# Transformer block on one core: where the last weight pieces stand in the load queue, and o's and LN2's transposes one visit later

## The chip, the core and the metric

One Trainium2 chip, one of its cores. The time is device microseconds (us) for one run of the whole program, from inputs in HBM to the output in HBM. Matmuls run on TensorE (PE, with its weight loads PEld), elementwise work on VectorE (DVE) and ScalarE (ACT), a few small operations on GpSimd (POOL); SyncE (SP) issues nearly all transfers. A transfer issued by SP goes to one queue over 16 DMA engines.

## The reference

S = 2048 rows of D = 576, 32 heads of 18, MLP width F = 4608, bfloat16 inputs.

```python
def _A_ref(x, wqkv, wo):
    qkv = (x @ wqkv).reshape(B, S, 3, H, Dh)            # q, k, v
    idx = pos[:, None] - (arange(8) * 2)[None, :]         # 8 keys, two rows apart, causal
    logits = einsum("bhsd,bhswd->bhsw", q, k[idx]) * Dh ** -0.5   # -1e9 where idx < 0
    return einsum("bhsw,bhswd->bhsd", softmax(logits), v[idx]).reshape(B, S, D) @ wo

def _B_ref(x, w1, b1, w2, b2):
    return gelu(layernorm(x) @ w1 + b1) @ w2 + b2

h = x + _A_ref(layernorm(x), wqkv, wo)
h2 = h + _B_ref(layernorm(h), w1, b1, w2, b2)
```

## The kernel before

**Tiles.** Row p*16 + j of x lies in partition p of tile j, so the 16 tiles of 128 rows are strided, and the keys of a tile are whole other tiles of the same parity (with the first rows taken from one partition further up, the "halo"). EVEN is tiles 0, 2, ... 14, ODD is 1, 3, ... 15. Attention runs over A = 14, 12, 10, 8, 6, 4, 2, 0, 15, ... in pairs (GROUPS): 14 and 12 are the first MLP group, 10 and 8 the second.

**A visit.** PE works in visits. One visit computes two "duos", a duo being the product of one tile with 576 columns. Each has a first phase (10 matmuls of 64 rows, in which two halves of the array take the two halves of the rows) and a second (8 matmuls with the halves exchanged). `visit` (L242) runs the first phases of all duos, then `hook`, then for each duo its second phase, its evacuation (`evac`, on ACT), and what `between` gives for it. Between the two phases of a duo stands a `marker` (L237): a nop on POOL that waits for the last matmul of the first phase, and for which the second phase waits. The PSUM pairs of the duos turn in a ring of three (tags C, A, B); the fourth, D, is for transposes and for W_o.

**The QKV stage.** 24 visits, numbered qd = 0 to 23, take `seq`: K and V and Q of the even tiles, then of the odd ones. `hooks[qd]`, `between[qd]`, `after[qd]` and `loads[qd]` (L937 to L983) say what each engine gets around a visit. The order on every engine is the order in which the code calls things (manual_schedule), so an entry moved in these tables is moved in the engines' queues. `wo_with` puts W_o's product of a tile into a visit as a third duo, in D.

**What is interleaved.** For tiles 14 and 12, attention is finished inside this stage: products of q with 8 K tiles (`att_qk_a`, L352, one DVE operation of 2.5 us), sums over the head dimension (`att_qk_add`, L361, four halvings), logits, maximum (`att_max`), exp on ACT, probabilities (`att_den`), products with V (`att_pv_a`, L407) and their sums (`att_pv_b`, L413, L414) into q_all, which then holds o. `halo(j, 1)` and `halo(j, 2)` (L347) reload a K or V tile of kv_ring, shifted, from DRAM once the products of tile j have read it; the products of the next tile read it too. `o_tail` copies o's last 64 columns on ACT, `tr_o` (L431) transposes o on PE, W_o's product follows, and `ln2` (h = x + W_o's product, statistics; DVE), `ln2_rstd` (the power −1/2, POOL, L161), `ln2_norm` (ACT, L539 and L174) and `tr_h` (PE, copied to hnT on ACT, L557) prepare the MLP's input hnT. For tiles 10 and 8, o goes out to DRAM and is read back transposed (`dma_tr_o`: L210, L211, L216) during the first MLP.

**Odd x.** Normalised odd tiles are written to q_all by ACT, sent out two at a time (`out_x`, L292 and L293) and read back transposed (`in_x`, L296) into xnT: read i serves tiles ODD[2i] and ODD[2i+1], visits 12 + 3i to 14 + 3i.

**Weights.** W1 comes in six pieces of 768 columns (768 KB each, `load_w1`), W_o in four pieces (`load_wo`, two transfers each), W2 in seven (`load_w2`) with the row blocks of 128 in the tuple. The last W2 block, rows 28 to 35, is w2b_sb. Every `load` waits for the last evacuation that was recorded before it (`pace`), and they all stand in SP's one queue with the stores and the transposed reads. The MLP visits of group 0 use W1's pieces in pairs: 0 and 1 in its visits 0 and 1, 2 and 3 in 1 and 2, 4 and 5 in visit 3.

**MLP.** For group 0 (`k == 0`, L1046 to L1056), `m1[v]` is called ahead of MLP visit v, `mid` within it, `ia[f]` and `ib[f]` ahead of row f of the second product (L603), for the first and the second tile. W_o's product for tile 10 (c) is the late duo of visit 3; that of tile 8 (d) stands at row 19 of the second product.

At the start PE multiplies constants (L833) so that it is not idle while x and the first weights come.

Of the kernel before, what the change touches and what calls it, by code (L numbers as in the profile page):

```python
# [17 lines left out]
def kernel(  # L18
# [12 lines left out]
    nc = tc.nc  # L31
    P = 128
# [11 lines left out]
    FA = 28  # L44
# [51 lines left out]
    def psum_pair(tag, name, dtype=F32):  # L96
        n = 512 if dtype == F32 else 1024
        return psum.tile([P, 2, n], dtype, tag=f"ps{tag}", name=name)
# [36 lines left out]
    def load_w2(c):  # L135
        f0, f1 = (0, 4, 7, 11, 14, 21, FA, FT)[c:c + 2]
        dst = w2a_sb[:, f0:f1, :] if f1 <= FA else w2b_sb[:]
        load(dst, B_w2[f0 * P:f1 * P, :].rearrange("(ft p) c -> p ft c", p=P))
# [79 lines left out]
    def half_rows(r):  # L218
        return slice(r * HP, (r + 1) * HP)
# [138 lines left out]
    def att_qk_add(j, steps):  # L358
        for o, a, c in steps:
            n = (c - a if c < 9 else 9) * H  # L360
            nc.vector.tensor_tensor(out=prod[:, :, o * H:o * H + n], in0=prod[:, :, a * H:a * H + n],  # L361
                                    in1=prod[:, :, c * H:c * H + n], op=ALU.add)

    def att_qk_b(j, i, skip=0):
        side[j] = i
        out = logit_of([j])[:, 0]
        att_qk_add(j, ((0, 0, 9), (0, 0, 4), (0, 0, 2), (0, 0, 1))[skip:])
        nc.vector.tensor_tensor(out=out, in0=prod[:, :, 0:H], in1=prod[:, :, 8 * H:9 * H], op=ALU.add)
        if j // 2 + 1 < W:
            nc.vector.memset(out[0:1, j // 2 + 1:W, :], -1e9)  # L370
# [332 lines left out]
    def c_(fn, *a):  # L703
        return lambda: fn(*a)
# [100 lines left out]
    with tc.manual_schedule(engines={ENG.PE, ENG.Activation, ENG.DVE, ENG.SP, ENG.Pool}):  # L805
# [26 lines left out]
        for n in [512] * 8 + [P] * 5:  # L832
            nc.tensor.matmul(busy[:, 0, 0:n], lhsT=ones[:, 0:P], rhs=ones[:, 0:n], start=True, stop=True)  # L833
# [104 lines left out]
        for c, v in enumerate((2, 3, 4, 13, 13, 17)):  # L938
            loads[v] = loads.get(v, []) + [c_(load_w1, c)]
        for q, v in enumerate((6, 8, 11, 12)):  # L940
            loads[v] = [c_(load_wo, [q])]
        for n, v in enumerate((19, 19, 20, 20, 21, 22)):
            loads[v] = loads.get(v, []) + [c_(load_w2, n)]
# [15 lines left out]
            13: [c_(ln1_act, 10, 1), c_(in_x, 2), c_(out_x, 3), c_(store_halo, A[2]), c_(store_halo, A[3])],  # L959
            14: [c_(att_pv, A[1]), c_(in_x, 3), c_(load, b2_bc, B_b2.partition_broadcast(P))],  # L960
            15: [c_(halo, A[1], 2), c_(o_tail, A[0])],
            17: [c_(o_tail, A[1]), c_(ln2, A[0]), c_(att_qk_a, A[2])],
            18: [c_(ln2_rstd, A[0]), c_(halo, A[2], 1)],
            19: [c_(ln2, A[1])],
            20: [c_(ln2_rstd, A[1]), c_(att_qk_rest, A[2], 0)],
# [4 lines left out]
            18: {1: [c_(tr_o, A[1], "D")]},  # L970
            19: {1: [c_(ln2_norm, A[0])]},
            21: [c_(ln2_norm, A[1])],
            22: [c_(att_exp, A[2])],
        }
        wo_with = {17: A[0], 19: A[1]}
# [5 lines left out]
            21: c_(tr_h, A[0], "D"),  # L981
            22: c_(tr_h, A[1], "D"),
# [6 lines left out]
        tr_x(EVEN[0], "D")  # L989
        for qd in range(len(seq) // 2):  # L990
            duos = [qkv_duo(*seq[2 * qd]), qkv_duo(*seq[2 * qd + 1])]
            if qd in wo_with:
                duos.append(wo_duo(wo_with[qd], "D"))
            visit(duos, hooks.get(qd), between.get(qd, ()), apart=qd == 0)
            call(after.get(qd, ()))
            call(loads.get(qd, ()))
# [37 lines left out]
        for k, g in enumerate(GROUPS):  # L1034
# [11 lines left out]
            if k == 0:  # L1046
                m1[0] += [c_(halos, 1), c_(load_w2, 6), c_(att_qk_a, d), c_(att_qk_rest, d, 1), c_(halo, d, 1)]
                mid[0] = {1: [c_(exps, d)]}
                m1[1] = [c_(pv_t, c), c_(pv_t, d), c_(add_b2, g[0]), c_(add_b2, g[1]), c_(att_qk_a, e), c_(halo, e, 1)]
# [109 lines left out]
```

## Time and profile before

| | |
|---|---|
| time, median of 3 | 361.98 us (361.90, 361.98, 363.82) |
| profiled execution | 362.23 us, span 360.4 us, granted clock 0.995 |
| PE busy | 352.6 us, 98% of the span |
| DVE busy | 295.9 us, 82% |
| ACT busy | 235.9 us, 65% |
| HBM | 23.38 MB read, 12.42 MB written, 99 GB/s over the span |
| QKV stage | to 68.15 us, the first matmul of the MLP |
| MLP group 0 | 68.15 to 106.3 us |

The windows view gives, for a stretch a:b, its length, then the busy time of PE, PEld, DVE, ACT and POOL with the number of instructions, the granted share of the TensorE clock, the busy share of the DMA engines and the rate in GB/s. The chain that ended last is PE for 80% of the span; the rest is DVE 11%, DMA 5%, ACT 2%:

| engine, line | what | share of the span |
|---|---|---|
| PE L228 | MLP's first product | 39% |
| PE L691 | second product, groups 2 to 7 | 25% |
| PE L603 | second product, groups 0 and 1 | 10% |
| PE L228 | W_o | 4% |
| DMA | transposed read of odd x (xnT) | 3% |

### The profile page before, as it was taken

Reading aid. Unit: us, or ns where it says so; the run is one execution under the profiler, and the core shown is the slowest. Engines: PE = TensorE matmul, PEld = TensorE weight load, DVE = VectorE, ACT = ScalarE, POOL = GpSimd, SP = SyncE. Lnnn points to the kernel's source line nnn. Section 1 sums busy time; section 2 is a strip of 40 time slices with the busy share of each in tenths; the row PEclk is TensorE's granted clock in tenths of the full one; section 3 lists DMA queues with packets and bytes.
Section 4 is the critical chain, followed back from the end, with each engine's and each line's share of the span. In section 5 each row is a group of like instructions: output and inputs, shape, how many; then the busy total and the mean of one; then the engine's idle time right before and its main releaser. Section 6 shows DMA issues by size and latency. Waiting matters only on the chain.

```text
span 360.4 us, 11550 instructions
## 1 busy us (share of the span) xinstructions
PE 352.6 (98%) x4938; PEld 290.7 (81%) x4938; DVE 295.9 (82%) x416; ACT 235.9 (65%) x524; POOL 48.1 (13%) x61
## 2 busy tenths in 40 slices
PE   7999998999999999999999999999999999999996
PEld 3788886788778877887788778877887788778874
DVE  5999999989889998998799899989998989520431
ACT  4889764898556783668656956695669566706620
POOL 2340005000212020201110202021102110210000
PEclk8999999999999999999999999999999999999999
DMA  7996599972636496732463355344545254283001
GB/s 240 329 294 193 147 258 310 367 253 55 169 66 100 132 244 109 129 79 51 91 102 90 85 124 84 90 86 120 88 90 99 58 85 58 54 120 51 4 1 34
DMA packets 63492, 46.29 MB, mean 128 GB/s; under 512 B 32192, under 2 KB 61760, under 8 KB 63440
## 3 DMA queue, kind: packets, MB, share of 16 engines
q1 hardware_dynamic: 59472, 41.50, 43.6%
q0 software_dynamic: 3744, 3.84, 9.9%
q8 instruction: 38, 0.62, 0.8%
q10 hardware_dynamic: 224, 0.22, 0.3%
q14 instruction: 14, 0.11, 0.1%
HBM read 23.38 MB, written 12.42 MB: 99 GB/s over the span
## 4 chain that ended last, share of the span: by engine, by line
PE 80%; DVE 11%; DMA 5%; ACT 2%; issue 1%; SPq 0%; DVEq 0%; ACTq 0%
PE pm L228 39%; PE po L691 25%; PE po L603 10%; PE pw L228 4%; DMA xnT<-xd 3%; DVE ln_stats L148 2%; DVE prod L361 2%; DVE prod L407 1%; DVE prod L352 1%; PE pq L228 1%; DMA x_all<-in_A_x_dram 1%; DMA wq_sb<-in_A_wqkv_dram 1%; ACT h_all L584 1%; DVE prod L413 1%; DVE ln_mv L149 1%
## 5 line engine op out<-in xcount | busy, mean ns | idle before, releaser
L228 PE MATMUL pm<-hnT,w_sb 64*128 64x256 bf16 x2304 | 143.0, 269 | 0.0
L584 ACT ACTIVATE h_all<-pm,b_sb 128x256 f16<-128x256 f32 (+1 forms) x288 | 108.7, 496 | 51.0 <-PE pm L228 50.3
L228 PEld LDWEIGHTS <-w_sb 64*128 64x128 bf16 x2304 | 111.6, 94 | 15.2 <-issue 1.7
L228 PE MATMUL pq<-wq_sb,xnT 64*128 64x288 bf16 x720 | 55.7, 286 | 3.0 <-DMA xnT<-xd 1.8
L691 PEld LDWEIGHTS <-h_all 128*128 128x128 f16 x480 | 46.2, 98 | 13.7 <-issue 1.6
L228 PEld LDWEIGHTS <-xnT 64*128 64x128 bf16 x864 | 44.7, 95 | 11.9 <-DMA xnT<-xd 2.1
L361 DVE TENSOR_TENSOR prod<-prod 128x2304 bf16<-128x2304 bf16 (+1 forms) x64 | 44.2, 691 | 2.1
L352 DVE TENSOR_TENSOR prod<-kv_ring,q_all 128x4608 bf16<-128x4608 bf16 x16 | 40.8, 2551 | 3.2 <-POOL ln_rstd L498 2.4
L407 DVE TENSOR_TENSOR prod<-kv_ring,probs 128x4608 bf16<-128x4608 bf16 x16 | 40.9, 2558 | 2.2 <-DMA kv_ring<-kv_dram 1.7
L228 PE MATMUL pm<-hnT,w1h_sb 64*128 64x256 bf16 x288 | 39.2, 269 | 0.0
L691 PE MATMUL po<-w2a_sb,h_all 128*128 128x288 bf16 (+1 forms) x262 | 35.9, 286 | 0.0
L413 DVE TENSOR_TENSOR prod<-prod 128x2304 bf16<-128x2304 bf16 (+1 forms) x32 | 33.9, 1058 | 1.1
L603 PEld LDWEIGHTS <-h_all 128*128 128x128 bf16 x288 | 27.9, 98 | 7.9 <-issue 0.9
L691 PEld LDWEIGHTS <-kv_ring 128*128 128x128 f16 x252 | 24.6, 98 | 6.3
L603 PE MATMUL po<-w2a_sb,h_all 128*128 128x288 bf16 x224 | 28.5, 286 | 0.0
L228 PE MATMUL pq<-wqh_sb,xnT 64*128 64x288 bf16 x144 | 28.1, 288 | 0.0
L793 POOL DMA_DIRECT2D x_all<-o_sb x12 | 10.7, 888 | 125.1 <-PE pw L228 72.3
L498 POOL TENSOR_TENSOR ln_rstd<-ln_var,mhalf 128x1 f32<-128x1 f32 x13 | 10.2, 786 | 84.2 <-ACT ln_var L497 84.2
L161 POOL TENSOR_TENSOR ln_rstd<-ln_veps,mhalf 128x1 f32<-128x1 f32 (+2 forms) x14 | 14.1, 1019 | 45.4 <-DVE ln_nmean L487 28.0
L691 PE MATMUL po<-w2b_sb,h_all 128*128 128x288 bf16 (+1 forms) x122 | 19.7, 286 | 0.2 <-DVE h_all L671 0.2
L228 PE MATMUL pw<-wo_sb,oT 64*128 64x288 bf16 x256 | 19.5, 283 | 0.0
L671 DVE TENSOR_TENSOR kv_ring<-h_all 128x1536 f16<-128x1536 f16 (+3 forms) x9 | 6.8, 760 | 15.4 <-ACT h_all L584 15.3
(113 smaller groups left out, 400.3 us busy)
## 6 DMA issues: line engine op xcount, KB each, us to landing
w_sb<-in_B_w_dram SPq DMA_DIRECT2D x6, 768.0 KB, 6.3
kv_ring<-kv_dram SPq DMA_DIRECT2D x28, 144.0 KB, 2.4
kv_dram<-kv_ring SPq DMA_DIRECT2D x13, 288.0 KB, 4.3
x_all<-in_B_b_dram SPq DMA_DIRECT2D x15, 144.0 KB, 3.8
w2a_sb<-in_B_w_dram SPq DMA_DIRECT2D x2, 1008.0 KB, 7.1
td<-q_all SPq DMA_DIRECT2D x14, 144.0 KB, 2.3
td<-hn SPq DMA_DIRECT2D x14, 144.0 KB, 1.8
x_all<-h POOLq DMA_DIRECT2D x14, 144.0 KB, 4.5
```

The source lines that it names most:

```text
L148: nc.vector.bn_stats(out=stats[:, i, c, :], in_=src[:, c * HALF:(c + 1) * HALF])
L161: nc.gpsimd.tensor_tensor(out=rstd[:], in0=veps[:], in1=mhalf[:].to_broadcast([P, n]), op=ALU.pow)
L228: last = nc.tensor.matmul(duo["g"][r ^ swap][i], lhsT=lhsT, rhs=rhs, start=(swap == 0 and i == 0 and kt == 0), stop=(swap == 1 and kt == K ...
L352: ins = nc.vector.tensor_tensor(out=prod[:], in0=k_ring[j % 2], in1=q_all[:, j, :].unsqueeze(1) .to_broadcast([P, W, D]), op=ALU.mult).ins
L361: nc.vector.tensor_tensor(out=prod[:, :, o * H:o * H + n], in0=prod[:, :, a * H:a * H + n], in1=prod[:, :, c * H:c * H + n], op=ALU.add)
L407: nc.vector.tensor_tensor(out=prod[:].rearrange("p w (d h) -> p w d h", h=H), in0=v_ring[j % 2].rearrange("p w (d h) -> p w d h", h=H), in ...
L413: nc.vector.tensor_tensor(out=prod[:, 0:n, :], in0=prod[:, 0:n, :], in1=prod[:, n:2 * n, :], op=ALU.add)
L498: ins = nc.gpsimd.tensor_tensor(out=rstd[:], in0=var[:], in1=mhalf[:], op=ALU.pow).ins
L584: pace[0] = nc.scalar.activation(out=hT(grp)[:, f, 0:N], in_=ps[:, r, i * N:(i + 1) * N], func=ACT.Gelu_apprx_tanh, bias=b1_sb[:, f:f + 1] ...
L603: nc.tensor.matmul(banks[half], lhsT=hT(grp)[:, f, i * P:(i + 1) * P], rhs=w2_rows(f)[:, half * HALF:(half + 1) * HALF], start=(f == 0), s ...
L691: nc.tensor.matmul(bank, lhsT=l, rhs=r, start=start, stop=stop, skip_group_check=True)
L793: nc.gpsimd.dma_start(out=x_of(j), in_=o_of.pop(j), accum_op=ALU.add)
```

## The change

The diff below is the whole of it. It moves W1's fourth piece from behind visit 13's stores to directly behind the third odd read, and pieces five and six behind the fourth odd read (and the load of b2). W_o's third piece goes from visit 11 to 8, its fourth from 12 to 11. W2's first two pieces become one, loaded behind visit 17, the next three go behind visits 19, 20 and 21, the fifth behind 22, and w2b_sb comes in two halves: the first where the whole one was, the second in the MLP's visit 1 behind the reload of V for tile 8. To make room for the latter, `pv_t(d)` is written out. The tail copy, the transpose and W_o's product of tile 12, its LN2, and the transposes of both tiles' LN2 come one visit later. The powers are called between a visit's duos, behind its markers, and no longer after the visit. Two of the four halvings of tile 10 stand ahead of tile 12's LN2 on DVE. At the start, PE gets three more short products of constants, and twelve of half the rows behind the first transposes.

```diff
@@ -133,8 +133,8 @@
         load(w1_sb[:, :, cols], B_w1[0:KF * P, cols].rearrange("(k p) c -> p k c", p=P))
 
     def load_w2(c):
-        f0, f1 = (0, 4, 7, 11, 14, 21, FA, FT)[c:c + 2]
-        dst = w2a_sb[:, f0:f1, :] if f1 <= FA else w2b_sb[:]
+        f0, f1 = (0, 7, 11, 14, 21, FA, 32, FT)[c:c + 2]
+        dst = w2a_sb[:, f0:f1, :] if f1 <= FA else w2b_sb[:, f0 - FA:f1 - FA, :]
         load(dst, B_w2[f0 * P:f1 * P, :].rearrange("(ft p) c -> p ft c", p=P))
 
 
@@ -361,10 +361,12 @@
             nc.vector.tensor_tensor(out=prod[:, :, o * H:o * H + n], in0=prod[:, :, a * H:a * H + n],
                                     in1=prod[:, :, c * H:c * H + n], op=ALU.add)
 
+    ADDS = ((0, 0, 9), (0, 0, 4), (0, 0, 2), (0, 0, 1))
+
     def att_qk_b(j, i, skip=0):
         side[j] = i
         out = logit_of([j])[:, 0]
-        att_qk_add(j, ((0, 0, 9), (0, 0, 4), (0, 0, 2), (0, 0, 1))[skip:])
+        att_qk_add(j, ADDS[skip:])
         nc.vector.tensor_tensor(out=out, in0=prod[:, :, 0:H], in1=prod[:, :, 8 * H:9 * H], op=ALU.add)
         if j // 2 + 1 < W:
             nc.vector.memset(out[0:1, j // 2 + 1:W, :], -1e9)
@@ -829,7 +831,7 @@
         load_w1h()
         busy = psum_pair("D", "busy")
         ones = nc.const_aps.tensor(1.0, [P, 512], BF16)
-        for n in [512] * 8 + [P] * 5:
+        for n in [512] * 8 + [P] * 8:
             nc.tensor.matmul(busy[:, 0, 0:n], lhsT=ones[:, 0:P], rhs=ones[:, 0:n], start=True, stop=True)
         nc.gpsimd.memset(mhalf[:], -0.5)
         nc.gpsimd.memset(eps2[:], EPS * EPS)
@@ -935,12 +937,10 @@
             ln2_ins(c, d)
 
         loads = {}
-        for c, v in enumerate((2, 3, 4, 13, 13, 17)):
-            loads[v] = loads.get(v, []) + [c_(load_w1, c)]
-        for q, v in enumerate((6, 8, 11, 12)):
-            loads[v] = [c_(load_wo, [q])]
-        for n, v in enumerate((19, 19, 20, 20, 21, 22)):
-            loads[v] = loads.get(v, []) + [c_(load_w2, n)]
+        for v, fns in ((2, [(load_w1, 0)]), (3, [(load_w1, 1)]), (4, [(load_w1, 2)]), (6, [(load_wo, [0])]), (8, [(load_wo, [1, 2])]),
+                       (11, [(load_wo, [3])]), (14, [(load_w1, 4), (load_w1, 5)]), (17, [(load_w2, 0)]), (19, [(load_w2, 1)]),
+                       (20, [(load_w2, 2)]), (21, [(load_w2, 3)]), (22, [(load_w2, 4)])):
+            loads[v] = [c_(*fn) for fn in fns]
         after = {
             0: [c_(ln1_even, 3), c_(ln1_even, 4)],
             1: [c_(ln1_even_rstd, 2, 3), c_(ln1_even, 5)],
@@ -956,30 +956,30 @@
             10: [c_(att_pv, A[0]), c_(ln1_act, 9, 1), c_(in_x, 1), c_(halo, A[1], 1)],
             11: [c_(out_x, 2), c_(halo, A[0], 2)],
             12: [c_(ln1_act, 10, 0)],
-            13: [c_(ln1_act, 10, 1), c_(in_x, 2), c_(out_x, 3), c_(store_halo, A[2]), c_(store_halo, A[3])],
+            13: [c_(ln1_act, 10, 1), c_(in_x, 2), c_(load_w1, 3), c_(out_x, 3), c_(store_halo, A[2]), c_(store_halo, A[3])],
             14: [c_(att_pv, A[1]), c_(in_x, 3), c_(load, b2_bc, B_b2.partition_broadcast(P))],
             15: [c_(halo, A[1], 2), c_(o_tail, A[0])],
-            17: [c_(o_tail, A[1]), c_(ln2, A[0]), c_(att_qk_a, A[2])],
-            18: [c_(ln2_rstd, A[0]), c_(halo, A[2], 1)],
-            19: [c_(ln2, A[1])],
-            20: [c_(ln2_rstd, A[1]), c_(att_qk_rest, A[2], 0)],
+            17: [c_(ln2, A[0]), c_(att_qk_a, A[2])],
+            18: [c_(halo, A[2], 1), c_(att_qk_add, A[2], ADDS[:2])],
+            20: [c_(ln2, A[1]), c_(att_qk_rest, A[2], 0, 2)],
         }
         between = {
             10: [c_(att_exp, A[0])],
             13: [c_(att_exp, A[1])],
-            18: {1: [c_(tr_o, A[1], "D")]},
-            19: {1: [c_(ln2_norm, A[0])]},
-            21: [c_(ln2_norm, A[1])],
+            18: [c_(o_tail, A[1])],
+            19: {0: [c_(ln2_rstd, A[0])], 1: [c_(ln2_norm, A[0])]},
+            21: {0: [c_(ln2_rstd, A[1])], 1: [c_(ln2_norm, A[1])]},
             22: [c_(att_exp, A[2])],
         }
-        wo_with = {17: A[0], 19: A[1]}
+        wo_with = {17: A[0], 20: A[1]}
         hooks = {
             0: {1: lambda: call([c_(tr_x, EVEN[1], "C"), c_(ln1_even, 2)])},
             **{n: {m: c_(tr_x, EVEN[2 * n + m - 1], "D" if m == 1 else None) for m in (1, 2)} for n in (1, 2, 3)},
             12: c_(tr_b1, "D"),
             16: c_(tr_o, A[0], "D"),
-            21: c_(tr_h, A[0], "D"),
-            22: c_(tr_h, A[1], "D"),
+            19: c_(tr_o, A[1], "D"),
+            22: c_(tr_h, A[0], "D"),
+            23: c_(tr_h, A[1], "D"),
         }
         seq = [(j, t) for t in (1, 2) for j in EVEN[:2]] + [(j, 1) for j in EVEN[2:]] \
             + [(j, 0) for j in A[0:2]] + [(j, 2) for j in EVEN[2:]] + [(j, 0) for n in (0, 4, 2) for j in EVEN[n:n + 2]] \
@@ -987,6 +987,10 @@
 
         ln1_even_rstd(0, 1)
         tr_x(EVEN[0], "D")
+        busy = psum_pair("B", "busy")
+        for n in range(12):
+            sl = half_rows(n % 2)
+            nc.tensor.matmul(busy[:, n % 2, 0:P], lhsT=ones[sl, 0:P], rhs=ones[sl, 0:P], start=True, stop=True)
         for qd in range(len(seq) // 2):
             duos = [qkv_duo(*seq[2 * qd]), qkv_duo(*seq[2 * qd + 1])]
             if qd in wo_with:
@@ -1044,9 +1048,10 @@
             if k == 2:
                 m1[3].insert(0, c_(out_store, GROUPS[1][0]))
             if k == 0:
-                m1[0] += [c_(halos, 1), c_(load_w2, 6), c_(att_qk_a, d), c_(att_qk_rest, d, 1), c_(halo, d, 1)]
+                m1[0] += [c_(halos, 1), c_(load_w2, 5), c_(att_qk_a, d), c_(att_qk_rest, d, 1), c_(halo, d, 1)]
                 mid[0] = {1: [c_(exps, d)]}
-                m1[1] = [c_(pv_t, c), c_(pv_t, d), c_(add_b2, g[0]), c_(add_b2, g[1]), c_(att_qk_a, e), c_(halo, e, 1)]
+                m1[1] = [c_(pv_t, c), c_(att_den, d), c_(att_pv_a, d), c_(halo, d, 2), c_(load_w2, 6), c_(att_pv_b, d),
+                         c_(dma_tr_o, d), c_(add_b2, g[0]), c_(add_b2, g[1]), c_(att_qk_a, e), c_(halo, e, 1)]
                 late_wo = wo_duo(c, "B")
                 ia[0] = [c_(ln2_h, c), c_(ln2_act, c), c_(put_b2, c), c_(halos, 2), c_(ln2_send, c), c_(att_qk_b, e, 0)]
                 ia[19] = [lambda d=d: wo_visit((d, "A"), fill=True), c_(ln2_h, d), c_(ln2_act, d), c_(put_b2, d), c_(ln2_in, c),
```

## The prediction

> **What bounds the kernel now.** First the page's busy line, then the windows of ten microseconds, which say where PE is not full.
>
> ```profile
> PE 352.6 (98%) x4938; PEld 290.7 (81%) x4938; DVE 295.9 (82%) x416; ACT 235.9 (65%) x524; POOL 48.1 (13%) x61
> 0.00:10.00 10.00, 7.55 (x61) 3.76 (x61) 5.61 (x19) 4.51 (x9) 1.85 (x10) 0.85 0.81 249
> 50.00:60.00 10.00, 8.54 (x145) 7.17 (x140) 9.69 (x18) 6.26 (x12) 4.21 (x2) 1.00 1.07 282
> 60.00:70.00 10.00, 9.44 (x166) 7.44 (x168) 9.01 (x15) 7.04 (x12) 0.31 (x1) 1.00 1.08 379
> ```
>
> PE is idle 7.8 us of 360.4: 2.5 in the first ten, about 3 behind 340, and 1.46 + 0.56 between 50 and 70, where the DMA share is over 1: the queue is full there. From 70 to 340 it has no gap, so that stretch can only move as a whole. What stops PE between 50 and 70, and what stood ahead of that transfer in SP's queue, the timelines of PE and SP show (start, duration, instruction; in brackets the idle time before it):
>
> ```profile
> 60.44 0.66 PE L228 MATMUL pq<-wq_sb,xnT 64*128 64x288 bf16 x8 [1.75 <-DMA xnT<-xd]
> 45.18 1.40 SPq L296 DMA_TRANSPOSE xnT<-xd  x1
> 46.63 0.58 SPq L292 DMA_DIRECT2D xd<-q_all  x1
> 47.77 1.03 SPq L306 DMA_DIRECT2D kv_dram<-kv_ring  x2
> 48.84 2.00 SPq L104 DMA_DIRECT2D w_sb<-in_B_w_dram  x2
> 51.01 3.86 SPq L296 DMA_TRANSPOSE xnT<-xd  x1
> ```
>
> The fourth odd x read is issued at 51.01 behind two W1 pieces of 768 KB, holds SP for 3.86 us and lands 9.4 us after its start, at 60.40; the other three took 3.6 to 3.8. PE's visit 21 waits for it.
>
> DVE is the other chain. It has no wait over 0.3 us from 10.5 to 63, then two for reloads of kv_ring, and its product for tile 8 ends in the transposed o that W_o's product takes:
>
> ```profile
> 63.60 2.56 DVE L352 TENSOR_TENSOR prod<-kv_ring,q_all 128x4608 bf16<-128x4608 bf16 x1 [0.47 <-DMA kv_ring<-kv_dram]
> 79.77 2.56 DVE L407 TENSOR_TENSOR prod<-kv_ring,probs 128x4608 bf16<-128x4608 bf16 x1 [0.97 <-DMA kv_ring<-kv_dram]
> 88.74 1.21 SPq L216 DMA_TRANSPOSE oT<-td  x1
> 91.80 0.66 PE L228 MATMUL pw<-wo_sb,oT 64*128 64x288 bf16 x8
> ```
>
> The transposed read took 2.9 us from start to landing for the tile before, so this one lands near 91.65: PE takes it 0.15 us later. Whatever PE wins before 70 it can keep only as far as this read moves too.
>
> **The change part by part.**
>
> *W1's pieces, and W_o's.* W_o's third piece moves from visit 11 to visit 8, the fourth from 12 to 11. Two issues (0.4 us each) enter SP ahead of the second odd read (36.41, then about 36.9, landing 40.5; visit 15 begins near 42.3, so this costs nothing) and two leave the stretch ahead of the third, which goes from 45.18 to about 44.2. The fourth W1 piece follows it, then the store of the last odd x. One W1 piece took 2.0 us of a full queue (landings 55.60 and 57.59, from issue plus time to landing). The third read lands near 47.9, the piece 49.9, the store 0.9 later, and the fourth read can be issued at about 51.0, with one piece already through. It took 2.8 us of the queue behind the pieces (57.59 to 60.40), and the two K/V stores ahead of it end near 52.4: landing 55.2, at most 57 if the piece and the stores share badly. Visit 21 wants it near 58.2. Of the 1.75 us all goes; below that nothing is won. The two pieces behind it are due at MLP visit 3, above 78.
>
> *o's and LN2's transposes a visit on.* Between visits 18 and 19 PE's starts pause 0.31 us (52.54 to 52.85) for o of tile 12, whose copy L199 ends at 52.46. In the hook of visit 19 it is long there: −0.31. W_o's product for 12 (1.1 us) moves from visit 19 to 20, its LN2 behind it. PE's sum: from 52.54, two visits of 2.22, transposes 0.14, W_o 1.1, so visit 21 starts near 58.2 and not 60.44. From there to the MLP at 68.15 it was 7.71 us with 0.28 of waiting for hn (64.28 to 64.56); 7.43 puts the MLP at 65.65 without a new wait. One is there: DVE takes LN2 of 12 behind two of tile 10's additions (2.1 us, 56.53 to 58.63, by which time W_o is through), veps is ready at 60.7, and on ACT the norm stands ahead of the copy of hnT and the evacuations of visit 22, in order. How long the power takes, two rows tell:
>
> ```profile
> 54.17 2.86 POOL L161 TENSOR_TENSOR ln_rstd<-ln_veps,mhalf 128x1 f32<-128x1 f32 x1 [26.38 <-DVE ln_nmean L487]
> 58.65 1.66 POOL L161 TENSOR_TENSOR ln_rstd<-ln_veps,mhalf 128x1 f32<-128x1 f32 x1 [1.62 <-DVE ln_nmean L487]
> ```
>
> Undisturbed it takes 0.55 to 0.75 (the late ones of L498). The first ended 0.46 behind DVE's L352 of 54.06, the second 0.39 behind the first addition of 58.55 (1.37 us). In the new place a short addition (0.44) begins beside it: end near 61.55, norm 1.17 → 62.75, copy 0.63 → 63.4, evacuation 0.6 → 64.0. The second duo of visit 23 wants that bank at 63.65: +0.35 (0 if the power is undisturbed, 0.8 if a second addition holds it). The MLP then starts near 66.0: **2.15 us earlier**, ends 1.7 and 2.5.
> That hold is what the Trainium skill, SBUF — State Buffer, "SBUF: two separate sides", calls an exclusive lock on a port pair: a DVE operation with two SBUF inputs and a GpSimd operation that reads SBUF exclude each other whole. The trace agrees (2.86 and 1.66 against 0.55). The rule lets whoever starts first win, so it also allows a worse order, the third rival below.
>
> *Powers behind markers.* The nops of POOL that release PE's second phases no longer queue behind a power waiting for veps. I count 0: no matmul of 50 to 70 has a POOL wait in brackets. The cover is the other duo's first phase (0.6 us); gone, it would cost what one marker did at 10.06, where a weight load waited 0.64 for it.
>
> *W2's pieces and the halves.* The K reload of tile 10, for which DVE waited 0.47, is now behind four x read, b2, two W1 pieces, V of 12 and seven W2 rows: 55.2 + 0.25 + 4.0 + 0.4 + 2.65 (1.03 MB at the 379 GB/s of the window) + 0.44 = 62.9, against 63.57 before; DVE wants it at 63.1. −0.45, ends −0.48 and +1.5 (SP held as at 51.01). The V reload of tile 10 was issued at 74.79 behind 1152 KB of w2b and took 4.9 instead of the 2.2 of an empty queue; now 576 KB and earlier: the 0.97 goes, ends 0 and 0.97. Together tile 8's o is ready 1.4 us sooner, 83.6. The other half of w2b is issued ahead of its store, at 81.4, 1.5 us of queue, out by 84.0. The store took 3.5 us (2.6 for tile 10), the read 2.9: 89.0 to 90.2. PE comes at 91.80 − 2.15 = 89.65. So +0 to 0.5 of new waiting, taken as 0.25. Rows 32 to 35 of W2 are used from 93 on and cost nothing.
>
> *Fill at the start.* Three more 128-column matmuls (0.06 each) end before q_all is ready at 4.77; twelve half-row ones, six pairs of 0.06 at full clock or 0.12 at half, lie in PE's 0.72 us gap before 5.87. The clock was 0.50 from 6.93 to 10.35, after a window in which PE was busy 1.78 of 3.41 us; with 0.5 us more it may stay whole, which would bring PE some 1 us ahead at 10.3. But visit 16 transposes o of tile 14, written by DVE at 45.51 and copied by ACT until 45.84, and PE reached that at 45.90 without idling. DVE does not depend on it, so PE would wait there: 0, ends 0 and −0.1.
>
> **Sum.** −1.75 − 0.31 − 0.28 + 0.35 (rounding of the visits' ends makes 2.15 of 2.0) and +0.25 at 89.65: **−1.9 us**. Behind that point DVE itself waits for PE (L473 at 93.82, 0.87), so both chains move together to the end. The profiled execution is 362.23 (span 360.4 and 1.8 around it), giving 360.3; it lies 0.25 above the median of 361.98, from which I forecast 360.1.
>
> **Rivals.**
> 1. *Given back at W_o's product of tile 8.* If seven W2 rows push the K reload to 64.5 or the store is slow beside w2b's half, o lands at 91 and PE, early, waits 1.4. For: the slack of 0.15, the full queue. Against: the 0.97 that falls away. Gain 0.2 to 1.0: 361.4.
> 2. *The x read is not freed.* Its store is now behind a W1 piece; if that costs 3 us more than reckoned the read lands at 58 to 60 and PE waits as before, and only the 0.31 stays: 361.7. Against it: every odd read without two pieces ahead took 3.6 to 3.8.
> 3. *Slower: the power of tile 12 misses its place.* If POOL gets the port neither at 61.2 nor between tile 10's last small operations, it is held by the product for tile 8, which runs 63.1 to 65.65: power 66.1, norm 67.3, copy 67.9, evacuation 68.5, then 0.6 + 0.38 + 1.0 of PE: the MLP at 70.5, 2.35 late: 364.3. It decides once the power has not begun by 63.1. It is the lock of that page, worked out on these rows; against it, the 1.66 row got in between two additions.
> 4. *More.* PE's early lead survives at 45.9 in part and the store takes 2 us: gain 2.4 to 3: 359.3.
>
> **Chances.** Forecast (359.6 to 360.8) 0.62; rival 1 0.16; rival 2 0.06; rival 3 0.06; rival 4 0.10. Of the forecast's cases six in ten win over 1.81 us, 0.5%, about what a measurement of this kernel can tell from no change: faster 0.37 + 0.10 = 0.47; slower 0.06 and 0.02 for what I do not see; the rest 0.45. The range leaves out rival 3 and the ends of 4: 359.2 to 361.9.
>
> **What will show it.** Right: no PE wait for xnT before visit 21, the fourth read landing under 57; a wait of some 0.3 us of PE for ACT in visit 23; the MLP's first pm near 66.0; no DVE wait for kv_ring at 79; the wait for o of tile 8 under 0.5 us. Wrong: a power of over 2 us behind 60.7, a K reload landing behind 64, or a wait of PE over 1 us at W_o near 90.

## The result, and the profile after

| | before | changed |
|---|---|---|
| time, median of 6 runs each | 362.00 us (361.84 to 363.82) | 366.82 us (366.12 to 367.36) |
| profiled execution | 362.23 us, span 360.4 us | 366.27 us, span 364.2 us |
| first matmul of the MLP | 68.15 us | 65.60 us |
| DVE's first product for tile 8 (L352) | 63.60 us | 68.34 us |
| DVE's product with V for tile 8 | 79.77 us | 83.58 us |
| W_o's product of tile 8 on PE | 91.80 us | 95.36 us |

The ratio is 1.0122 (95%: 1.0100 to 1.0145): 1.2% slower. PE won more of the early stage than predicted, 2.55 us where 2.15 were forecast, and DVE lost 4.74 us within the same stage. W_o's product of tile 8 needs both, and it follows the later one. In the two profiled executions it starts 3.56 us later and the end comes 4.04 us later; between the medians it is 4.82, and what follows explains the profiled ones.

First the windows of the changed kernel (start and end, length, then busy time of PE, PEld, DVE, ACT, POOL, the clock, the DMA share and GB/s).

```profile
50.00:60.00 10.00, 10.00 (x173) 8.08 (x170) 9.69 (x16) 5.91 (x12) 2.86 (x1) 1.00 0.83 222
60.00:70.00 10.00, 9.92 (x184) 8.47 (x180) 4.26 (x10) 8.59 (x17) 0.73 (x1) 1.00 1.07 386
70.00:80.00 10.00, 8.53 (x158) 7.61 (x154) 9.55 (x14) 7.55 (x18) 0.00 (x0) 1.00 0.77 276
80.00:90.00 10.00, 7.49 (x119) 6.17 (x115) 9.72 (x12) 7.58 (x22) 0.00 (x0) 1.00 0.46 122
```

Before, PE was busy 8.54 and 9.44 us in the first two windows and had no gap behind 70; now it is full to 70 and idle 1.5 and 2.5 us in the next two. DVE fell from 9.01 to 4.26 us in the second. The timelines of DVE, PE and POOL in the changed kernel show the waits (idle time before the instruction in brackets, with what ended it):

```profile
68.34 2.56 DVE L352 TENSOR_TENSOR prod<-kv_ring,q_all 128x4608 bf16<-128x4608 bf16 x1 [5.50 <-DMA kv_ring<-kv_dram]
83.58 2.56 DVE L409 TENSOR_TENSOR prod<-kv_ring,probs 128x4608 bf16<-128x4608 bf16 x1
65.60 0.60 PE L228 MATMUL pm<-hnT,w_sb 64*128 64x256 bf16 x8
79.03 0.61 PE L228 MATMUL pm<-hnT,w_sb 64*128 64x256 bf16 x8 [1.47 <-ACT h_all L586]
87.09 0.66 PE L228 MATMUL pw<-wo_sb,oT 64*128 64x288 bf16 x8 [2.13 <-DMA oT<-td]
95.36 0.67 PE L228 MATMUL pw<-wo_sb,oT 64*128 64x288 bf16 x8 [1.37 <-ACT ln_var L499]
60.46 0.73 POOL L161 TENSOR_TENSOR ln_rstd<-ln_veps,mhalf 128x1 f32<-128x1 f32 x1 [3.74 <-DVE ln_nmean L489]
```

DVE stands 5.50 us for the K reload of tile 10, where it stood 0.47. The other reload wait, 0.97 us at the product with V, is gone, so 4.74 us of lateness become 3.81. PE then meets the lateness in three places: behind an exp that waits for tile 8's logits (79), at o of tile 10 (87), and at W_o's product of tile 8 (95). The last is named for ACT, but the transposed read of tile 8's o was issued at 92.53; with the 2.8 us that the read for tile 10 took it lands at 95.3. What stands behind the first of the three is in ACT's timeline, the exp for tile 8:

```profile
75.59 0.42 ACT L395 ACTIVATE logits<-logits 128x256 f32<-128x256 f32 x1 [2.40 <-DVE logits L377]
```

The chain of waits, in order of time, puts the reload at its head:

```profile
57.73 0.69 DVE prod L361
58.42 0.34 DVE h L475
58.76 9.55 DMA kv_ring<-kv_dram
68.34 2.57 DVE prod L352
70.93 1.37 DVE prod L361
```

Why the reload took 9.55 us stands in SP's timeline of the changed kernel, and in one row of SP's waits (us in total, times, longest):

```profile
43.95 1.32 SPq L296 DMA_TRANSPOSE xnT<-xd  x1
45.36 0.53 SPq L104 DMA_DIRECT2D w_sb<-in_B_w_dram  x1
45.99 0.46 SPq L292 DMA_DIRECT2D xd<-q_all  x1
46.50 0.47 SPq L293 DMA_DIRECT2D xd<-q_all  x1
47.01 2.82 SPq L306 DMA_DIRECT2D kv_dram<-kv_ring  x2
53.49 1.33 SPq L296 DMA_TRANSPOSE xnT<-xd  x1
54.92 0.99 SPq L104 DMA_DIRECT2D x_all<-in_B_b_dram  x1
55.97 0.97 SPq L104 DMA_DIRECT2D w_sb<-in_B_w_dram  x2
56.98 0.50 SPq L347 DMA_DIRECT2D kv_ring<-kv_dram  x1
57.53 0.69 SPq L104 DMA_DIRECT2D w2a_sb<-in_B_w_dram  x1
58.76 2.31 SPq L347 DMA_DIRECT2D kv_ring<-kv_dram  x1
```

```profile
SPq L296 <- DMA xd<-q_all: 3.5, 1, 3.5
```

W1's fourth piece is issued at 45.36, behind the third read, and lands 7.01 us later; the two stores of the last odd x behind it land at 53.12 and 53.36. The fourth read reads what they wrote, so SP waits for them, and SP issues in order: from 49.83 to 53.49 it puts nothing into the queue. What was in the queue runs out. In the stretch from 53 to 59 us it moved 273 GB/s in the kernel before and 132 in the changed one:

```profile
53.00:59.00 6.00, 5.69 (x100) 4.93 (x94) 5.83 (x13) 4.23 (x9) 3.21 (x2) 1.00 1.14 273
```

```profile
53.00:59.00 6.00, 6.00 (x108) 4.78 (x104) 5.86 (x8) 4.23 (x8) 2.86 (x1) 1.00 0.73 132
```

Then everything is issued within 5.3 us, with the K reload last: b2 landed at 59.67, W1's last two pieces at 62.38 and 64.46, V of tile 12 at 64.85, W2's seven rows at 67.89, the K reload near 68.3.

### The profile page after: what moved, and what is told of

Its sections match the earlier page's. It is cut to its first block, busy times and chain, and to the rows that moved or that the text cites. A ratio compares the mean times of both kernels' runs of the same rounds, so it can differ in the third digit from the quotient of the medians.

```text
span 364.2 us, 11580 instructions
## 1 busy us (share of the span) xinstructions
PE 353.9 (97%) x4953; PEld 289.2 (79%) x4953; DVE 296.0 (81%) x416; ACT 235.8 (65%) x524; POOL 47.1 (13%) x61
## 4 chain that ended last, share of the span: by engine, by line
PE 70%; DVE 20%; DMA 5%; ACT 2%; SPq 1%; issue 1%; DVEq 0%; ACTq 0%
PE pm L228 33%; PE po L693 25%; PE po L605 8%; PE pw L228 4%; DVE prod L352 3%; DVE prod L361 3%; DVE prod L409 3%; DVE ln_stats L148 3%; DMA kv_ring<-kv_dram 3%; DVE prod L415 2%; DMA x_all<-in_A_x_dram 1%; ACT h_all L586 1%; SPq L104 1%; DMA oT<-td 1%; DVE ln_mv L149 1%
## 5 line engine op out<-in xcount | busy, mean ns | idle before, releaser
L693 PEld LDWEIGHTS <-h_all 128*128 128x128 f16 x480 | 46.2, 98 | 13.7 <-issue 1.6
L228 PE MATMUL pq<-wq_sb,xnT 64*128 64x288 bf16 x720 | 54.5, 283 | 0.3
L228 PEld LDWEIGHTS <-xnT 64*128 64x128 bf16 x864 | 42.2, 94 | 11.0 <-ACT xnT L283 0.8
L352 DVE TENSOR_TENSOR prod<-kv_ring,q_all 128x4608 bf16<-128x4608 bf16 x16 | 40.8, 2551 | 8.2 <-DMA kv_ring<-kv_dram 5.5
L228 PEld LDWEIGHTS <-oT 64*128 64x128 bf16 x288 | 13.6, 94 | 8.2 <-DMA oT<-td 4.5
```

Source lines behind the costliest of these rows:

```text
L228: last = nc.tensor.matmul(duo["g"][r ^ swap][i], lhsT=lhsT, rhs=rhs, start=(swap == 0 and i == 0 and kt == 0), stop=(swap == 1 and kt == K ...
L352: ins = nc.vector.tensor_tensor(out=prod[:], in0=k_ring[j % 2], in1=q_all[:, j, :].unsqueeze(1) .to_broadcast([P, W, D]), op=ALU.mult).ins
L693: nc.tensor.matmul(bank, lhsT=l, rhs=r, start=start, stop=stop, skip_group_check=True)
```

## The experiments

Two theories were set against each other. **T**: the loss is DVE's wait for the K reload of tile 10, handed on through o of tiles 10 and 8 to the end; three changes feed it: A, W1's fourth piece ahead of the last odd store (it stops SP); B, W2's seven rows ahead of the reload; C, W1's last two pieces ahead of it. **R**: PE starts the MLP so early that ACT and DVE, which serve it and the attention at once, cannot follow, whatever the loads do.

The experiments ran on three chips: e1 to e6, f1 and f2 on one, f3 and f4 on another, and g0 ("before, again") and g1 on a third. There the kernel before had medians of 360.6 to 361.9 us, so each ratio is to runs of it on the same chip. The profiled executions at a glance (us; waits of DVE in parentheses):

| run | MLP starts | L352 of tile 8 | product with V, tile 8 | W_o of tile 8 | profiled time | ratio (95%) |
|---|---|---|---|---|---|---|
| before | 68.15 | 63.60 (0.47) | 79.77 (0.97) | 91.80 | 362.23 | |
| before, again | 67.49 | 62.92 (0.23) | 78.75 (0.62) | 91.14 | 361.51 | 0.9989 (0.9967 to 1.001) |
| changed | 65.60 | 68.34 (5.50) | 83.58 | 95.36 | 366.27 | 1.0122 (1.01 to 1.0145) |
| e1: B undone | 66.49 | 65.67 (1.94) | 80.92 | 92.36 | 363.30 | 1.0073 (1.0045 to 1.01) |
| e2: B, C undone | 65.99 | 63.15 | 80.86 (2.51) | 92.80 | 363.37 | 1.0041 (1.0016 to 1.0066) |
| e3: A undone | 65.88 | 66.38 (3.28) | 81.63 | 93.54 | 364.28 | 1.0093 (1.0059 to 1.0127) |
| e4: before + A, C | 66.21 | 65.41 (2.86) | 82.13 (1.51) | 92.27 | 363.18 | 1.0057 (1.0024 to 1.0089) |
| e5: before + o, LN2 | 66.41 | 63.56 | 78.92 (0.17) | 90.73 | 361.13 | 1.0011 (0.9987 to 1.0034) |
| e6: before + W2 | 68.11 | 66.18 (2.92) | 81.42 | 93.15 | 363.55 | 1.007 (1.0046 to 1.0095) |
| f1: e2, W2's tail later | 65.54 | 62.67 | 77.89 | 92.12 | 363.36 | 1.0109 (1.0068 to 1.0149) |
| f2: f1, no fill | 65.98 | 62.95 | 78.20 | 94.01 | 367.12 | 1.0145 (1.0115 to 1.0176) |
| f3: A, B, C undone | 65.72 | 62.86 | 78.39 (0.32) | 89.89 | 360.89 | 1.0002 (0.9983 to 1.0021) |
| f4: f3, w2b later | 65.57 | 62.72 | 77.97 | 89.22 | 360.26 | 0.9982 (0.9959 to 1.0006) |
| g1: f4, no fill | 65.69 | 62.84 | 78.07 | 89.56 | 362.44 | 1.0028 (1.0003 to 1.0053) |

The profiled time is that of one execution; the medians were 362.76 for e2, 364.33 for f1 and 366.49 for f2. From W_o's product of tile 8 to the end it is 270.4 to 271.2 us in every row but f2 and g1, which are taken up below. So the profiled time is decided by when that product starts.

**e1, W2's rows behind the K reload.** The changed kernel with the load moved one visit on:

```diff
-                       (11, [(load_wo, [3])]), (14, [(load_w1, 4), (load_w1, 5)]), (17, [(load_w2, 0)]), (19, [(load_w2, 1)]),
+                       (11, [(load_wo, [3])]), (14, [(load_w1, 4), (load_w1, 5)]), (18, [(load_w2, 0)]), (19, [(load_w2, 1)]),
```

> The changed kernel, with W2's first seven rows loaded behind visit 18 and not 17, so behind the K reload of tile 10 in SP's queue; nothing else. Theory T (the whole loss is the 5.5 us that DVE waits for that reload): W2's rows took 64.85 to 67.9 of the queue, so the reload lands near 65.3 and not 68.3, DVE waits some 2.5 us, 366.8 - 3.0 = 363.8. Rival R (the loss comes from PE starting the MLP 2.5 us ahead of ACT and DVE, its waits at 79, 87 and 95, and not from the reload): no change, 366.5 to 367.

The reload ends DVE's wait 2.67 us sooner (65.67), and W_o's product starts 3.00 sooner. PE's wait at 79 is gone although the MLP starts only 0.9 us later than in the changed kernel. The median, 363.49, is near the 363.8 that T had forecast.

**e2, W1's last two pieces behind it too.**

```diff
-                       (11, [(load_wo, [3])]), (14, [(load_w1, 4), (load_w1, 5)]), (17, [(load_w2, 0)]), (19, [(load_w2, 1)]),
+                       (11, [(load_wo, [3])]), (18, [(load_w1, 4), (load_w1, 5), (load_w2, 0)]), (19, [(load_w2, 1)]),
```

> The changed kernel, with W1's fifth and sixth pieces and W2's first rows all behind visit 18, so behind the K reload of tile 10. T: the reload has only the fourth x read, b2 and the V reload ahead of it and lands under 60.5, DVE takes it without a wait near 62.9, and with the MLP still starting near 65.6 the whole gains what the prediction had reckoned or a little less: 359.8 to 360.8, a wait of PE of about 0.5 us at W_o of tile 8. R: PE still ahead of ACT and DVE, 365 to 367.

The K reload lands at 61.15 and DVE does not wait for it. But the same bytes now stand ahead of the V reload, which the same chain needs 15 us after the K reload's product begins. DVE's timeline in e2:

```profile
63.15 2.55 DVE L352 TENSOR_TENSOR prod<-kv_ring,q_all 128x4608 bf16<-128x4608 bf16 x1
80.86 2.56 DVE L409 TENSOR_TENSOR prod<-kv_ring,probs 128x4608 bf16<-128x4608 bf16 x1 [2.51 <-DMA kv_ring<-kv_dram]
```

Of the 5.50 us 2.51 came back at the next reload: taking loads out of one reload's way is not enough while they stand in the next one's, in a queue that is still behind by what it lost between 53 and 59. T's mechanism held at the K reload, and its time, 359.8 to 360.8, did not: the median was 362.76.

**e3, W1's fourth piece behind the last odd store.**

```diff
-            13: [c_(ln1_act, 10, 1), c_(in_x, 2), c_(load_w1, 3), c_(out_x, 3), c_(store_halo, A[2]), c_(store_halo, A[3])],
+            13: [c_(ln1_act, 10, 1), c_(in_x, 2), c_(out_x, 3), c_(load_w1, 3), c_(store_halo, A[2]), c_(store_halo, A[3])],
```

> The changed kernel, with W1's fourth piece behind the store of the last odd x (and ahead of the K/V stores), nothing else. Theory A (that piece, 7.0 us to landing, held the store and so SP: the fourth read went out at 53.5 and not at 51, and everything behind it stood still): the read goes out near 49.5, lands at 54 to 56, the K reload lands at 63 to 65 and the time is 361 to 363.3. Theory B (the seven rows of W2 ahead of the reload are what counts, SP's wait nothing): the reload still lands over 67, 366 to 367.

The odd stores land at 50.6 and 50.8, SP waits 0.7 us for them and not 3.5, and the fourth read is issued at 50.91 and lands at 55.34: the prediction's own 51.0 and 55.2. The K reload comes only 1.96 us sooner, at 66.35, with C and B still ahead of it, between the two expectations (63 to 65 for A, over 67 for B); b2 lands 1.82 us behind the fourth read and W1's last two pieces 5.84 behind b2. W_o's product comes 1.82 sooner and the profiled time is 1.99 lower; the median, 364.08, lies above A's 361 to 363.3. The windows of e3 also show half clock, in the stretch behind a PE wait of 2.01 us for tile 10's o that ended at 85.03:

```profile
85.03:88.45 3.42, 3.42 (x32) 2.34 (x34) 3.35 (x6) 0.56 (x3) 0.00 (x0) 0.52 0.87 255
```

Half clock for 3.42 us is some 1.6 us of PE work (3.42 x 0.48); the changed kernel had no such stretch behind its wait of 2.13. It did not decide e3's time. The transposed read of tile 8's o was issued late too:

```profile
90.61 1.21 SPq L216 DMA_TRANSPOSE oT<-td  x1
```

With the 2.7 us that the read for tile 10 took in e3 it lands near 93.3, and PE took it at 93.54, so that a PE at full clock would have waited for it and won some 0.2 us at most.

**e4, the kernel before with W1's and W_o's order alone** (A and C, of the change's diff the two tables that load W1 and W_o).

```diff
+        for v, fns in ((2, [(load_w1, 0)]), (3, [(load_w1, 1)]), (4, [(load_w1, 2)]), (6, [(load_wo, [0])]), (8, [(load_wo, [1, 2])]),
+                       (11, [(load_wo, [3])]), (14, [(load_w1, 4), (load_w1, 5)])):
...
+            13: [c_(ln1_act, 10, 1), c_(in_x, 2), c_(load_w1, 3), c_(out_x, 3), c_(store_halo, A[2]), c_(store_halo, A[3])],
```

> The kernel before, with only the new places of W1's and W_o's pieces; W2, its halves, and o's and LN2's visits as before. T: PE's 1.75 us wait for x goes, but the K reload of tile 10 lands near 65.2 as it does in the changed kernel without W2's rows ahead of it, 1.6 us later than before, so W_o of tile 8 and all behind it is 1.5 us late: 363.2 to 364. R: the move by itself is a gain of what PE waited, 360.3 to 361.5.

The fourth read is issued at 53.71 and lands at 58.46: PE's wait for it falls to 0.38 us, the early start is there, and DVE waits 2.86 for K. Against the kernel before in its second profile (g0, 62.92, on another chip) the product starts 2.49 us later; against the first (63.60) 1.81.

**e5, the kernel before with o, LN2 and the powers alone** (the tables `between`, `wo_with`, `hooks` and entries 17 to 20 of `after`, as in the change).

```diff
+            18: [c_(o_tail, A[1])],
+            19: {0: [c_(ln2_rstd, A[0])], 1: [c_(ln2_norm, A[0])]},
+            21: {0: [c_(ln2_rstd, A[1])], 1: [c_(ln2_norm, A[1])]},
...
+        wo_with = {17: A[0], 20: A[1]}
```

> The kernel before with only the o and LN2 transposes a visit on, the powers of LN2 behind the markers and the residual additions ahead of LN2 of tile 12; loads and fill as before. Theory T: no load moves, so the K reload of tile 10 lands near 63.6 us as before and DVE waits no more than before; visit 21's wait for x stays; time within 0.3 us of before (ratio 0.999 to 1.000). Rival (these moves bring the loss, by an ACT chain that ends later): ratio 1.004 or more.

No measurable difference: this part costs nothing and wins nothing by itself. The fourth read landed at 58.56 in this run, not 60.4 as expected, and PE came to it without waiting.

**e6, the kernel before with W2's places and halves alone** (B).

```diff
-        for n, v in enumerate((19, 19, 20, 20, 21, 22)):
+        for n, v in enumerate((17, 19, 20, 21, 22)):
...
+                m1[1] = [c_(pv_t, c), c_(att_den, d), c_(att_pv_a, d), c_(halo, d, 2), c_(load_w2, 6), c_(att_pv_b, d),
+                         c_(dma_tr_o, d), c_(add_b2, g[0]), c_(add_b2, g[1]), c_(att_qk_a, e), c_(halo, e, 1)]
```

> The kernel before with only W2's new places and halves: seven rows more ahead of the K reload of tile 10, so it lands near 66.2 us (2.65 us later than 63.57), and the V reload's wait of 0.97 us is gone: about 1.7 us later at the end, ratio near 1.0047. Rival (the seven rows alone are hidden, the loss needs the W1 piece ahead of the store): ratio within 0.001 of 1.

DVE's timeline in e6:

```profile
66.18 2.56 DVE L352 TENSOR_TENSOR prod<-kv_ring,q_all 128x4608 bf16<-128x4608 bf16 x1 [2.92 <-DMA kv_ring<-kv_dram]
81.42 2.56 DVE L407 TENSOR_TENSOR prod<-kv_ring,probs 128x4608 bf16<-128x4608 bf16 x1
```

Landing where theory T put it, 66.2, with the V wait gone; the rival is out, and R with it, since here the MLP starts at 68.11, as late as before, and the loss is 0.7%. The two halves of the change add up, as far as profiles of several chips can be added: 62.92 + 2.49 (e4) + 3.26 (e6) = 68.7, where the changed kernel has 68.34.

**f1, e2 with W2's last rows behind the read of tile 10's o; f2, the same without the fill at the start.** Of f1:

```diff
-                m1[1] = [c_(pv_t, c), c_(att_den, d), c_(att_pv_a, d), c_(halo, d, 2), c_(load_w2, 6), c_(att_pv_b, d),
-                         c_(dma_tr_o, d), ...
+                m1[1] = [c_(pv_t, c), c_(load_w2, 4), c_(load_w2, 5), c_(att_den, d), c_(att_pv_a, d), c_(halo, d, 2), c_(att_pv_b, d),
+                         c_(dma_tr_o, d), c_(load_w2, 6), ...
```

> The changed kernel with W1's fifth and sixth pieces and W2's first seven rows behind the K reload of tile 10 (as in e2), and with W2's rows 21 to 27 and 28 to 31 issued behind the transposed read of tile 10's o, rows 32 to 35 behind that of tile 8's o. Theory T (the loss is one wait for a reload, handed on 1:1 through tile 10's o to W_o of tile 8): with fewer bytes ahead of it the V reload of tile 10 lands near 76.7 us, before DVE wants it at 78.35; o of tile 10 lands near 81.6, that of tile 8 near 88.4, and PE waits at neither, so that the gain of the early stage (about 2.1 us at the MLP's start) reaches the end: ratio about 0.994. Rival: the late rows of W2 (row 21 is used near 91 us, row 28 near 93.5) or the read of o behind the V reload take the wait's place: ratio 1.000 or above, with a PE wait over 1 us between 80 and 96.

> f1 with the start's short products as they were in the kernel before (five in place of the twelve half-row ones). Theory: the fill is worth nothing, since PE waits near 45.5 us for q_all of tile 14, so the time is that of f1 within 0.1 us, with a PE wait near 45 us that is as much shorter as PE is later. Rival: half clock near 7 to 10 us costs up to 1 us that is not given back.

Both of T's landings held (V reload 76.67, o of tile 10 81.39, no DVE wait), and the kernel is slower all the same: the forecast for tile 8's o, 88.4, was 3.7 us off. SP's timeline in f1, from the load of W2's row 21 on, and the PE row that pays for it:

```profile
79.87 0.53 SPq L104 DMA_DIRECT2D w2a_sb<-in_B_w_dram  x1
80.49 0.51 SPq L104 DMA_DIRECT2D w2b_sb<-in_B_w_dram  x1
81.09 0.46 SPq L347 DMA_DIRECT2D kv_ring<-kv_dram  x1
83.15 0.36 SPq L210 DMA_DIRECT2D td<-q_all  x1
83.56 0.66 SPq L211 DMA_DIRECT2D td<-q_all  x1
89.22 1.21 SPq L216 DMA_TRANSPOSE oT<-td  x1
```

```profile
92.12 0.66 PE L228 MATMUL pw<-wo_sb,oT 64*128 64x288 bf16 x8 [2.87 <-DMA oT<-td]
```

Tile 8's o is ready and its write issued at 83.15, 5.7 us ahead of the changed kernel, but eleven rows of W2 are in front of it: it lands at 89.16, and SP cannot issue the transposed read before. It is mechanism A again, a store behind a weight piece with a read that waits for it. f1's ratio, 1.0109, is more than this profile (363.36, clock 0.999) accounts for: three of its six runs had a mean granted clock of 0.991 to 0.995 and took 364.97 to 367.21 us, and none of these was profiled. f2, forecast within 0.1 us of f1, missed that by 2.2 us (medians): the same wait was 4.23 us, since the read was issued 1.89 us later, and the clock fell behind it. Why the read is later without the fill is not shown. Windows of f2:

```profile
90.00:95.00 5.00, 0.99 (x10) 0.58 (x10) 1.24 (x4) 1.16 (x2) 0.67 (x1) 0.80 0.38 82
95.00:100.00 5.00, 5.00 (x28) 2.49 (x25) 2.38 (x4) 1.59 (x4) 0.00 (x0) 0.51 0.86 293
```

From W_o's product to the end f2 takes 273.1 us in place of 270.4 to 271.2: some 2.5 us of PE work (5.00 x 0.49) went in the second of these windows.

**f3, all three undone at once** (the diffs of e2 and e3 together); **f4, f3 with both halves of w2b behind the read of tile 8's o.** Of f4, beyond f3:

```diff
-                m1[0] += [c_(halos, 1), c_(load_w2, 5), c_(att_qk_a, d), c_(att_qk_rest, d, 1), c_(halo, d, 1)]
+                m1[0] += [c_(halos, 1), c_(att_qk_a, d), c_(att_qk_rest, d, 1), c_(halo, d, 1)]
...
-                m1[1] = [..., c_(halo, d, 2), c_(load_w2, 6), c_(att_pv_b, d), c_(dma_tr_o, d), ...
+                m1[1] = [..., c_(halo, d, 2), c_(att_pv_b, d), c_(dma_tr_o, d), c_(load_w2, 5), c_(load_w2, 6), ...
```

> The changed kernel with all three causes taken away at once: W1's fourth piece behind the last odd store (as in e3), and W1's fifth and sixth pieces and W2's first seven rows behind the K reload of tile 10 (as in e2). Theory T: the queue is not left empty for some 2 us near 53 to 55 us, so the backlog ahead of the V reload of tile 10 (landed near 80.8 in e2) is 2.1 us shorter: it lands near 78.7, DVE waits at most 0.7 for it, PE waits nothing at tile 10's o; tile 8's o still stands behind the last four rows of W2 and lands near 91, PE waits about 1 us there: ratio about 0.998 to 1.001. Rival: the fourth odd x read gets no earlier and the V reload lands as in e2: ratio 1.004.

> f3 with both halves of W2's last piece (rows 28 to 31, 32 to 35) behind the transposed read of tile 8's o, so that neither stands ahead of the V reload of tile 10 or of the write of tile 8's o. Theory T: the V reload lands near 77.2, before DVE wants it (near 78); tile 8's o is written near 85 and read near 88, before PE comes to W_o of tile 8 near 90: no wait over 0.3 us left between 66 and 90, the MLP's start about 2 us earlier than in the kernel before reaches W_o of tile 8, and the ratio is 0.995 to 0.998. Rival: row 28 (used near 93) is late in the place of o, with a PE wait over 1 us at W2, or LN2's transposes are late behind the two halves: ratio 1.000 or above.

f3 takes the whole loss away (1.0002): DVE waits 0.32 us for the V reload (to 78.39) and PE 0.45 for o of tile 8. f4 has no PE wait left between 46 and 100; its timelines of SP, DVE and PE:

```profile
50.44 1.77 SPq L296 DMA_TRANSPOSE xnT<-xd  x1
62.72 2.55 DVE L352 TENSOR_TENSOR prod<-kv_ring,q_all 128x4608 bf16<-128x4608 bf16 x1
77.97 2.56 DVE L409 TENSOR_TENSOR prod<-kv_ring,probs 128x4608 bf16<-128x4608 bf16 x1
89.22 0.66 PE L228 MATMUL pw<-wo_sb,oT 64*128 64x288 bf16 x8
```

Its median is 359.99 us beside 360.64 (12 and 23 runs). It beats the changed kernel by over 1% across chips; against the kernel before its interval still touches 1, so it may be anything from 0.4% faster to no faster. The forecast for it was 0.995 to 0.998.

**g0, the kernel before unchanged; g1, f4 without the fill.** The fill in question:

```diff
-        for n in [512] * 8 + [P] * 8:
+        for n in [512] * 8 + [P] * 5:
...
-        busy = psum_pair("B", "busy")
-        for n in range(12):
-            sl = half_rows(n % 2)
-            nc.tensor.matmul(busy[:, n % 2, 0:P], lhsT=ones[sl, 0:P], rhs=ones[sl, 0:P], start=True, stop=True)
```

> The kernel before, unchanged, profiled on the same chip as the other kernels here. Theory: fourth odd x read landed near 60.4 us, a PE wait near 1.75 us for it in visit 21, K reload near 63.6, a DVE wait near 1 us for the V reload, W_o of tile 8 between 90.5 and 91.8 us: with that the gain of f4 (W_o of tile 8 at 89.22) is 1.3 to 2.6 us by the profiles. Rival: on this chip the wait for x is under 1 us and the kernel before comes to W_o of tile 8 near 90 us, which is why f4 gains only 0.2% by the times.

> f4 with the start's short products as in the kernel before (five, and no half-row ones). Theory of the prediction (the fill is worth nothing, since PE waits near 45.3 us for q_all of tile 14): the time is f4's within 0.1%, and the PE wait of 0.24 us near 45.2 is gone or shorter. Rival: without the fill the clock is half in the slices near 7 to 10 us and PE comes out of the first stage later by up to 1 us, ratio 0.2 to 0.3% above f4's.

g0 has a wait for x of 1.53 us and W_o's product at 91.14: by the profiles f4 is 1.92 us ahead there, and 1.25 at the end. The 0.67 between is given back behind 89 us: by the first MLP matmul of each later group f4 is still 1.80 ahead near 214 us (213.92 beside 215.72) and 1.35 near 250 (250.16 beside 251.51), with a PE wait of 0.28 us at 232.68 that g0 does not have. The two profiles are of two chips.

g1 is a miss too: 1.0028 where f4 has 0.9982, each beside the kernel before on its own chip, and the intervals just overlap. It is not the clock of the rival, which was 1.00 from 3.4 to 13.7 us in g1 too. PE reaches W_o's product only 0.34 us later. But the transposed read of tile 8's o is issued at 86.55 and not 85.35, the next tile's K reload behind it lands at 95.19 and not 93.63 (DVE waits 1.91 us, in f4 0.70), and that lateness comes out in two PE waits that f4 does not have, 0.49 us for w2b at 94.83 and one in the next group:

```profile
144.32 0.61 PE L228 MATMUL pm<-hnT,w_sb 64*128 64x256 bf16 x8 [1.59 <-DMA hnT<-td]
```

The 0.34 and these two waits are 2.4 us, f4 loses 0.28 at its own wait of 232.68, and the two profiles lie 2.2 apart. The queue parts from f4's long before 85 us: the odd stores land at 48.6 and not 50.3, the fourth read is issued at 48.74 and not 50.44 but lands at 56.01 and not 54.87, and the V reload of tile 10 lands at 77.38 and not 76.59. Whether the missing fill does this, or the other chip, is not shown.

## Why the prediction was wrong

**The step that failed** is one term of the sum: "55.2 + 0.25 + 4.0 + 0.4 + 2.65 + 0.44 = 62.9", the landing of the K reload. It measured 68.3. Part by part: the fourth read landed at 57.50 (+2.30); b2 2.17 behind it and not 0.25 (+1.92); W1's two pieces 4.79 and not 4.0 (+0.79); V as said; seven rows of W2 3.04 and not 2.65 (+0.39). That is the 5.4. It fails first at the price of W1's fourth piece: 2.0 us, taken from two landings next to each other in a full queue. That is what a piece adds to those behind it when the queue is full; here it was not (56 GB/s from 47 to 48 us, 91 from 48 to 49), and what counted was the 7.01 us from issue to landing, for the stores behind it shared that time, and the fourth read could not be issued before they had landed. The prediction put that issue at "about 51.0"; it was 53.49. It named the piece and the stores as sharing badly ("at most 57") and let the answer stop at PE's visit 21, which had the slack. It did not carry the same lateness on to the five loads behind SP's stand, nor count the queue running empty. e3 shows this step alone: with the store first, 50.91 and 55.34.

e3 also shows that this is not all of the 5.4: with the read on time the reload still landed at 66.35, 3.4 us behind 62.9. The terms "0.25 + 4.0" for b2 and W1's two pieces, which are distances between landings in a full queue too, were 1.82 and 5.84 there and 2.17 and 4.79 in the changed kernel. So a second step failed with the first: distances from a full queue were used for transfers issued into one that was not full. What sets their time there stays open.

The rule that bears on it is in the Trainium skill, DMA: Bandwidth & Descriptors, "Anatomy of one DMA — SWDGE (gpsimd) path": a wait on a semaphore is done by the issuing sequencer ahead of the dispatch, and the DMA engines only work off their queues. That section describes GpSimd's path; for SP, which issues here, the trace agrees, with its 3.5 us.

**What was right.** The wait for x went although the read was late (no PE wait for xnT in the changed kernel), but only just: the read landed at 57.50, past the "under 57" given as a sign, and PE's visit 21 took it at 57.78. With landings at 58.46 (e4) and 58.07 (f1) PE waited 0.38 and 0.20 us. The MLP's start was forecast at 66.0 and came at 65.60; the +0.35 for the power did not come, since tile 12's took 0.73 us and ended at 61.19 with no large DVE operation beside it, so rival 3 is out too. That 65.60 is so near the 66.0 less the 0.35 is partly luck: e1 and e2, with the same early stage, start the MLP at 66.49 and 65.99. DVE wanted K at 62.84 (forecast 63.1). The fill left PE waiting 0.24 us at 45.26 for o of tile 14, as reckoned; f2 and g1 put its "0" in doubt. The powers behind markers, and o and LN2 a visit on, cost nothing (e5).

The 0.97 of the V reload went too, but this run does not show the reason given: DVE came to it 3.81 us later than before. Where DVE is on time it waits 0.32 us for it with half of w2b ahead (f3), and not at all with none ahead (f4).

**The rivals.** Rival 1 named the right place, the K reload and then W_o's product of tile 8, with 64.5 for the landing and 1.4 us of PE waiting; it was 68.3, and 5.35 us in five waits. At that size it no longer only gives back the gain: the +4.74 of DVE, less 0.97, overtakes it. Rival 2's mechanism, the store behind a W1 piece, was what happened, and its price of 3 us was nearly right (the read was issued 2.5 us late); it looked for the damage on PE, and it came on DVE. The two were priced apart and their sum was not: A with C loses 0.6% (e4), B alone 0.7% (e6).

**On the range.** "SP held as at 51.01" gave the reload +1.5 us as its upper end; the bound lacked a case in which SP waits for a store's landing, although the diff puts that store behind a load of 768 KB.

## What to carry to other kernels

A store that a later read waits for must not stand behind a large load in one in-order queue: price it by the load's time from issue to landing, not by its share of a full queue, and then move every transfer behind the read by that amount at least. When loads are moved past each other, write down the landing of each later one that some engine waits for, with the bytes ahead of it; in e2 and f1 the wait only moved from the K reload to the V reload to the write of o, and it went away only when what stood ahead of each of the three had landed by the time it was wanted (f4). An engine that gains time gains nothing where it meets the other chain: the place to look at first is the instruction that takes from both.

## What the runs showed of the hardware

- A W1 piece of 768 KB, issued alone behind a transposed read, took 7.01 us to land in the changed kernel and 5.6 to 5.9 in e3, f3 and f4, where a store was ahead of it; the two stores behind it took 7.1 and 6.9 us, though they are of 256 and 64 KB.
- The clock is granted at half behind a wait of PE, and not always: 4.23 us of waiting were followed by 0.51 from 95 to 100 us (f2), 2.01 us by 0.52 for 3.42 us (e3), while 2.13 (changed) and 2.87 us (f1) left it at 1.00. The Trainium skill, TensorE: Matmul & The Clock Gate, "What's actually happening", has half clock come back after at least one idle window of about 3.4 us. f2 and f1 agree; e3's 2.01 us is shorter than that (PE was busy 1.42 of the 3.43 us up to 85.03), and the measurement decides: a wait of 2 us can already be followed by half clock for 3.42 us.
- The clock after the start is whole with the fill (1.00 from 6.93 to 10.35 in the changed kernel, with PE busy 3.14 us of the 3.41 before) and also without it in g0 and g1 (2.80 of 3.41), though the first profile of the kernel before had 0.50 there (1.78 of 3.41). So a half clock there comes in some executions and not in others.
